# Attention and a low-rank mixer in one kernel: 128-row score operands for heads 0 and 1, two more crossbar transposes, and another order of steps

## The chip, the cores and the metric

The kernel runs on one core of a Trainium2 chip. The metric is the device time of one execution in microseconds, as the median of several runs of the same program. One further execution is recorded by the hardware profiler, and all views of the profile come from that one.

## The reference

The inputs are q, k, v with 8 batches, 8 heads, 576 positions and 64 features in fp32, a signal s for each batch, head and position, and four matrices: U (576x32), V (32x576), w_ch1 (512x2048) and w_ch2 (2048x512). The output is fp32, 8x576x512.

```
scores = q @ k.T / 8                          # per batch and head
cum    = cumsum(max(s, 0))
scores = where(causal, -1e9, scores + min(-(cum[i] - cum[j]), 0))
attn   = softmax(scores);   x = attn @ v      # heads side by side: 512 features
h = x.T @ U @ V                               # over positions, rank 32
u = x + h.T
out = u + max(u @ w_ch1, 0) @ w_ch2
```

## The kernel before

All matmuls are bf16. The work is 64 heads in 32 pairs (a pair is two heads, 128 features of x; a batch has four pairs), and nine groups of 512 tokens for the last two products. The order of all steps is written out by hand: a string `SEQ` of tokens for the first two batches (heads 0 to 15, pairs 0 to 7), whose part ahead of the bar also has warm-up matmuls, and a string `PAIR` that is played once for each pair from 8 on. Each engine executes its own instructions in the order in which the tokens issue them. The loads of the first two batches and the weights go through GpSimd in the order of `LOADS`.

What the tokens stand for, with the lines of the profile:

- `T`, `t` (heads 0 to 15): six TensorE transposes of a head's q and k into PSUM (L219), and two copies of it into the head's operand slot, by ScalarE (`tA`) or VectorE (`tV`) (L231). `G` (four parts for each group of four heads from head 16): VectorE transposes q or k (L245), and after every second part SP issues four copies, one per head, into the slot (L251). A slot holds four heads with 128 rows each: 64 features, four rows for the decays (copied by `R`, L169, or in the opening), and zeros. There are three slots.
- `D`, `E`: the score matmuls of a head on and below the diagonal (L261). For heads 0 and 1 they take 64 rows, and each is followed by a second matmul that adds the decays from another operand (L270). In the first batch a matmul with a triangle of large negative numbers masks the diagonal (L281). `d`, `f`, `m`, `l`: exponentials on ScalarE (L326). `k`, `K`: masks on VectorE by a minimum (L329), from head 8.
- `A`, `a`: attention times v, 15 matmuls (L340), and on VectorE the division (L355, L356).
- For a pair n: `U` multiplies x by U (L370), `u` copies that (L381), `Y` multiplies by V (L423), and `y` writes the piece u = x + h, transposed, into `uT`. x itself must be turned for that. Batches 0 and 1 turn x by matmuls with the identity into the same PSUM tile (`X`, L388, and L409 in `Y`), and `y` is a copy on either engine (L441). From batch 2, `x` turns it by a crossbar transpose that SP issues (L398), and `y` is a VectorE addition (L439).
- `F` feeds one unit of the last two products: `widen(g)` (16 units, each four 512-column matmuls with a tile of w_ch1, L459, and a ReLU by ScalarE, L466) and `narrow(g)` (16 units of four matmuls with w_ch2, L476; after four units one output tile is complete). `Q` puts these units into a queue. `r` does the next due copy: a ReLU, or the final step of an output tile. That final step adds u in token order. For group 0, four matmuls with the identity add it in PSUM (L488) and VectorE copies the tile (L500). For later groups `turn_u` has turned `uT` by a crossbar transpose from SP at the group's first unit (L444), and VectorE adds it (L502). SP then stores the tile (L508).
- `L` is one step of the decays of batches 4 to 7, `Z` clears buffers, `p` issues warm-up matmuls (L547), `e` is a feed that is played from pair 16 on.

In `PAIR` the numbers are relative to the pair: `D0` is the first head of this pair, `A-2` and `A-1` are the heads of the pair before, `U-2` and `Y-2` belong to two pairs before. `G1` works on the group that is used about two pairs later. When the last `y` of a batch is done, the units of that batch's group go into the queue.

PSUM has four buffers for scores and four for all else. Each load of GpSimd and each DMA of SP uses one of eight completion semaphores in turn.

Of the kernel before, what the change touches and what calls it, by code (L numbers as in the profile page):

```python
# [20 lines left out]
def kernel(  # L21
# [236 lines left out]
    def product(h, dst, j, lo, hi, start, stop):  # L258
        bias = bias_0 if h < 2 else None
        rows = D if bias else 128  # L260
        nc.tensor.matmul(  # L261
            dst,
            lhsT=head_of(h)[0:rows, ds(S + j * 128, 128)],
            rhs=head_of(h)[0:rows, lo:hi],
            start=start,
            stop=stop and not bias,
            skip_group_check=True,
        )
        if bias:
            nc.tensor.matmul(  # L270
                dst,
                lhsT=bias[0][:, ds(j * 128, 128)],
                rhs=bias[1 + h][:, lo:hi],
                start=False,
                stop=stop,
                skip_group_check=True,
            )
# [124 lines left out]
    def mix_out(n):  # L402
        mixed = n >= 2 * PB
        cut = 512 - 64 * (n // PB)
# [23 lines left out]
    def mix_done(copy, n):  # L428
        b, hp = divmod(n, PB)
        cut = 512 - 64 * b  # L430
        for got, lo, hi in mix_of.pop(n):
            for p, e in ((lo, min(hi, cut)), (max(lo, cut), hi)):
# [3 lines left out]
                dst = uT[:, at // 512 % 4, hp, ds(at % 512, e - p)]  # L436
                if b >= 2:
                    turned = xT[n % 3].rearrange("p t c -> p (t c)")
# [10 lines left out]
    hidden = {}  # L449
    UB = 1  # L450

    def widen(g):
        if g >= UB:
            turn_u(g)
# [15 lines left out]
    def narrow(g):  # L470
        hT = hidden.pop(g)
        for i in range(4):
            f2 = pwork()
            tok = g * 512 + i * 128
            for nf in range(NF):
# [4 lines left out]
                    start=(nf == 0),  # L480
                    stop=g >= UB and nf == NF - 1,
                    skip_group_check=True,
                )
                if nf % 4 == 3 and nf < NF - 1:
                    pending.append(None)
                    yield
            for dt in range(4 if g < UB else 0):
                nc.tensor.matmul(  # L488
                    f2[:, ds(dt * 128, 128)],
                    lhsT=uT[:, g % 4, dt, ts(i, 128)],  # L490
                    rhs=identity,
                    start=False,
                    stop=(dt == 3),
                    skip_group_check=True,
                )

            def finish(f2=f2, tok=tok, i=i):
                o_sb = work.tile([128, DM], FP32, tag="o_sb", name="o_sb", bufs=3)
                if g < UB:
                    nc.vector.tensor_copy(o_sb, f2)  # L500
                else:
                    nc.vector.tensor_tensor(  # L502
                        o_sb.rearrange("p (d c) -> p d c", d=4),
                        f2.rearrange("p (d c) -> p d c", d=4),
                        u_sb[g % 2][:, :, i, :],
                        op=ALU.add,
                    )
                nc.sync.dma_start(out=out_flat[ds(tok, 128), :], in_=o_sb)  # L508
# [45 lines left out]
    def prepare(i):  # L554
        if i == 0:
            for pT in pTs:
                nc.vector.memset(pT[:, :, 1600:], 1.0)
        elif i == 1:
            nc.vector.memset(slots[2][:D, :, 2 * S :], 0.0)
            nc.vector.memset(slots[2][D:, :, :], 0.0)  # L560
        else:
            nc.vector.memset(slots[0][D:, 0:2, :], 0.0)

    def queue(n):
# [20 lines left out]
        "X": mix_x,  # L585
        "x": turn_x,
        "Y": mix_out,
        "t": take,
# [40 lines left out]
    def opening():  # L629
# [28 lines left out]
        for slot in slots[:2]:  # L658
            nc.vector.memset(slot[:D, :, 2 * S :], 0.0)
        nc.vector.memset(slots[0][D:, 0:2, 2 * S :], 0.0)  # L660
        nc.vector.memset(v_slots[0][:, :, :, D : D + 1], 1.0)
# [49 lines left out]
    def begin_v(i):  # L711
# [14 lines left out]
    LOADS = (  # L726
        "u1 v0 u0 k0 w0 s0 w3 w2 w1 s1 x2 v1 x0 x1 x3 q4 v2 q5 "
    )

    SEQ = (  # L730
        "p7 p5 Z0 T0 tA0 tA0 p8 T3 T1 tA1 T2 tV3 D0 d0 tV3 tV2 tA1 p3 E0 D1 p2 d1 T5 f0 E1 tV2 "
        "m0 T6 f1 D2 T4 | m1 l0 tV5 E2 D3 tV6 d2 E3 f2 tV4 m2 tV4 l1 D4 A1 f3 tV5 A0 d3 E4 d4 "
        "T7 D5 m3 tA6 a1 d5 E5 f4 a0 m4 A2 U0 Z1 f5 m5 A3 D6 R2 uA0 tA7 a2 a3 X0 Y0 l2 tV7 A5 "
        "U1 A4 uV1 yA0 d6 D7 l3 X1 E6 Y1 d7 f6 m6 a4 a5 yV1 E7 U2 f7 A6 uV2 X2 a6 Y2 m7 yA2 A7 "
        "T8 T9 tA8 a7 U3 tV8 uA3 X3 Y3 yV3 D8 Q0 tV9 E8 F tA9 Z2 F d8 r R3 F r F r r T11 F F f8 "
        "r tA11 T10 F Q100 D9 r tV11 tV10 F r T13 k8 E9 T12 m8 F r L tA10 tV12 d9 r l4 k9 tV13 "
        "F K4 tV12 r f9 D10 d10 F F D11 m9 r r E10 f10 m10 l5 F F k10 r tV13 D12 T14 F r E11 "
        "d12 tV14 T15 r tA15 A9 A8 d11 F tV14 f11 k12 tA15 D13 m11 a9 a8 U4 k11 l6 r K5 F uV4 "
        "E12 X4 Y4 A11 f12 m12 E13 r F a11 f13 m13 D14 A10 a10 r D15 F d14 yV4 d13 R4 E14 d15 "
        "U5 F K6 uA5 l7 r X5 E15 k14 f14 F A12 r G4 Y5 k15 F r F k13 A13 f15 m15 a12 r F yA5 K7 "  # L740
        "m14 a13 A15 r U6 r uA6 a15 A14 G4 F r G4 F r F F a14 G4 r U7 F X6 r R5 Y6 L r L yA6 "
        "uA7 L F L F X7 Y7 L r r yA7 Q1 F F Q101 r r F r G5 L G5 L F L r "
    )
    PAIR = (
        "D0 E0 r d0 A-2 U-2 G1 r e k0 F a-2 G1 D1 r A-1 f0 uA-2 e r l0 d1 F m0 a-1 x-1 r F r E1 "
        "f1 k1 Y-2 r e K0 r yA-2 m1 F F "
    )
# [51 lines left out]
```

## Time and profile before

| | us |
|---|---|
| median of 5 runs (373.23 to 376.15) | 375.61 |
| the profiled execution | 376.15 |
| its span | 374.4 |
| TensorE busy | 365.1 |
| ScalarE busy | 210.7 |
| VectorE busy | 193.2 |
| GpSimd busy | 108.5 |

The span runs from the program's first instruction to its last, as the profiler sees it; the execution's own time holds a little more. The chain of work that ended last lies on TensorE for 73% of the span and on DMAs for 17%. A line of the profile names the engine, the line of the kernel, the operation, the tile that is written and the tiles that are read, the shape and the number of such instructions. PE is TensorE, DVE VectorE, ACT ScalarE, POOL GpSimd, SP SyncE.

### The profile page before, as it was taken

What the parts mean: (1) busy time and instruction counts of PE and PEld (TensorE: products, weight loads), DVE (VectorE), ACT (ScalarE), POOL (GpSimd) and SP (SyncE); (2) the same over time, 40 slices, a digit from 0 to 9 for tenths busy, and PEclk for the clock granted to TensorE, in tenths of its full rate; (3) what the DMA queues carried; (4) which work ended last, traced back from release to release, by engine and by line L of the source; (5) the groups of instructions that cost most, each with busy time, mean ns of one, the idle gap of its engine ahead of it and who ended that gap; (6) DMA issues with size and microseconds to landing.
All of it is one profiled execution on the core that took longest, in us unless ns stands there. A gap on an engine that the chain in (4) does not pass through costs nothing.

```text
span 374.4 us, 7894 instructions
## 1 busy us (share of the span) xinstructions
PE 365.1 (98%) x3119; PEld 206.0 (55%) x3119; DVE 193.2 (52%) x406; ACT 210.7 (56%) x429; POOL 108.5 (29%) x175
## 2 busy tenths in 40 slices
PE   8989999998899999999999999999999999999995
PEld 3566566654566565555555555555555544444442
DVE  8487566886478675665476546665343322011011
ACT  7596997178555686347733774377436711611710
POOL 8973338674454274063404400000000000000000
PEclk9999999999899999999999999999999999999999
DMA  7999999999999999869995994363224015005002
GB/s 89 153 196 207 162 164 128 159 182 201 154 140 191 197 149 148 124 125 141 139 149 106 172 115 80 95 161 47 56 76 102 19 46 140 2 28 140 2 28 84
DMA packets 108924, 44.89 MB, mean 120 GB/s; under 512 B 93440, under 2 KB 100640, under 8 KB 108888
## 3 DMA queue, kind: packets, MB, share of 16 engines
q0 software_dynamic: 65616, 18.43, 62.8%
q1 hardware_dynamic: 43272, 25.96, 35.3%
q8 instruction: 24, 0.39, 0.4%
q14 instruction: 12, 0.10, 0.1%
HBM read 37.51 MB, written 10.03 MB: 127 GB/s over the span
## 4 chain that ended last, share of the span: by engine, by line
PE 73%; DMA 17%; POOL 6%; DVE 3%; issue 1%; SPq 0%; DVEq 0%; POOLq 0%
PE pwork L476 29%; PE pwork L459 27%; DMA w_sb<-in_moe_w_ch_dram 10%; PE pscore L261 8%; PE pwork L340 6%; DMA slot<-turned 4%; PE pwork L370 2%; DVE turned L245 2%; POOL v_slot L142 2%; DMA v_slot<-in_v_dram 2%; PE pwork L423 2%; DMA qk_sd<-in_q_dram 1%; POOL hT L116 1%; POOL qk_sd L134 1%; POOL U_sb L691 0%
## 5 line engine op out<-in xcount | busy, mean ns | idle before, releaser
L326 ACT ACTIVATE pT<-pscore 128x512 bf16<-128x512 f32 (+1 forms) x224 | 113.3, 564 | 71.3 <-PE pscore L261 65.8
L459 PE MATMUL pwork<-uT,w_sb 128*128 128x512 bf16 x576 | 133.7, 380 | 0.0
L476 PE MATMUL pwork<-w_sb,hT 128*128 128x512 bf16 x576 | 132.5, 379 | 0.0
L466 ACT ACTIVATE hT<-pwork 128x512 bf16<-128x512 f32 x144 | 85.9, 612 | 55.9 <-PE pwork L459 55.4
L476 PEld LDWEIGHTS <-hT 128*128 128x128 bf16 x576 | 54.5, 98 | 58.1
L459 PEld LDWEIGHTS <-w_sb 128*128 128x128 bf16 x576 | 54.5, 98 | 57.5 <-issue 0.6
L261 PE MATMUL pscore<-slot 128*128 128x128 bf16 (+5 forms) x576 | 64.8, 241 | 3.1 <-DMA slot<-turned 2.3
L502 DVE TENSOR_TENSOR o_sb<-pwork,stage 128x512 f32<-128x512 f32 x32 | 21.9, 686 | 73.8 <-PE pwork L476 70.8
L261 PEld LDWEIGHTS <-slot 128*128 128x128 bf16 (+1 forms) x576 | 40.8, 98 | 32.0 <-DMA slot<-turned 3.1
L245 DVE STREAM_TRANSPOSE turned<-qk_sd 128x576 bf16<-128x576 bf16 x48 | 54.3, 1134 | 0.1
L134 POOL DMA_DIRECT2D qk_sd<-in_q_dram x48 | 27.1, 574 | 77.6 <-DVE turned L245 63.0
L329 DVE TENSOR_TENSOR pT<-pT,keep 128x512 bf16<-128x512 bf16 (+1 forms) x84 | 28.0, 352 | 37.4 <-ACT pT L326 36.1
L340 PE MATMUL pwork<-v_slot,pT 128*128 128x65 bf16 x960 | 40.0, 194 | 0.1
L340 PEld LDWEIGHTS <-pT 128*128 128x128 bf16 x960 | 35.5, 98 | 2.8 <-DVE x_sb L356 0.3
L356 DVE TENSOR_TENSOR x_sb<-pwork,rec 128x320 bf16<-128x320 f32 x64 | 31.5, 492 | 2.2
L439 DVE TENSOR_TENSOR uT<-pwork,stage 128x384 bf16<-128x384 f32 (+7 forms) x48 | 19.8, 452 | 22.1 <-PE pwork L423 14.3
L134 POOL DMA_DIRECT2D qk_sd<-in_k_dram x48 | 27.1, 571 | 11.6 <-DMA v_slot<-in_v_dram 6.1
L142 POOL DMA_DIRECT2D v_slot<-in_v_dram x32 | 28.2, 894 | 3.8 <-DMA w_sb<-in_moe_w_ch_dram 3.4
L355 DVE RECIPROCAL rec<-pwork 128x5 f32<-128x5 f32 x64 | 12.1, 189 | 24.2 <-PE pwork L340 24.0
L231 DVE COPY slot<-pwork 64x576 bf16<-64x576 bf16 x20 | 15.8, 799 | 11.9 <-PE pwork L219 7.3
L370 PE MATMUL pwork<-x_sb,U_sb 128*128 128x128 bf16 x160 | 14.5, 222 | 0.3 <-DVE x_sb L356 0.2
L423 PE MATMUL pwork<-V_sb,ux 128*128 128x512 bf16 (+6 forms) x64 | 13.1, 286 | 0.0
(80 smaller groups left out, 136.9 us busy)
## 6 DMA issues: line engine op xcount, KB each, us to landing
out_dram<-o_sb SPq DMA_DIRECT2D x36, 256.0 KB
slot<-turned SPq DMA_DIRECT2D x96, 72.0 KB
v_slot<-in_v_dram POOLq DMA_DIRECT2D x32, 128.0 KB, 8.8
w_sb<-in_moe_w_ch_dram POOLq DMA_DIRECT2D x8, 512.0 KB, 12.7
qk_sd<-in_q_dram POOLq DMA_DIRECT2D x48, 72.0 KB, 4.0
qk_sd<-in_k_dram POOLq DMA_DIRECT2D x48, 72.0 KB, 5.4
stage<-in_q_dram POOLq DMA_DIRECT2D x2, 288.0 KB, 10.6
stage<-in_k_dram POOLq DMA_DIRECT2D x2, 288.0 KB, 11.4
```

What stands on the lines that cost most here:

```text
L134: nc.gpsimd.dma_start(out=qk_t[g][ds(32 * a, 32), c, :].rearrange("p (n f) -> p n f", n=6), in_=src[g // 2, 4 * (g % 2) + a].rearrange("(n ...
L142: nc.gpsimd.dma_start(out=vt[:, t, :, 0:D], in_=v[b, :, ds(t * 128, 128), :].rearrange("h p d -> p h d"),)
L245: nc.vector.transpose(turned[:, e, c].rearrange("p (n m t) -> p n t m", n=6, t=3), src[:, c].rearrange("p (n t e d) -> p e n t d", n=6, t= ...
L261: nc.tensor.matmul(dst, lhsT=head_of(h)[0:rows, ds(S + j * 128, 128)], rhs=head_of(h)[0:rows, lo:hi], start=start, stop=stop and not bias, ...
L326: nc.scalar.activation(dst, src, EXP, scale=scale)
L329: nc.vector.tensor_tensor(p, p, m, op=ALU.min)
L340: nc.tensor.matmul(po[:, i, :], lhsT=p_of(h)[:, ds(spot(j, i), 128)], rhs=v_slots[h // H % 3][:, j, h % H, :], start=(j == 0), stop=(j == ...
L356: nc.vector.tensor_tensor(x_of[b][:, h % H // 2, :, ts(h % 2, D)], po[:, :, 0:D], rec.to_broadcast([128, 5, D]), op=ALU.mult,)
L370: nc.tensor.matmul(up[:, 0:128], lhsT=U_sb[:, t, :], rhs=x_part(n, t), start=(t == 0), stop=(t == 4), skip_group_check=True,)
L459: nc.tensor.matmul(f1, lhsT=w1_sb[nf // 4][:, kt, ds(nf % 4 * 128, 128)], rhs=uT[:, g % 4, kt, :], start=(kt == 0), stop=(kt == 3),)
L466: pending.append(lambda nf=nf, f1=f1: nc.scalar.activation(hT[:, nf, :], f1, RELU))
L476: nc.tensor.matmul(f2, lhsT=hT[:, nf, ds(i * 128, 128)], rhs=w2_sb[nf // 4][:, nf % 4, :], start=(nf == 0), stop=g >= UB and nf == NF - 1, ...
```

## The change

Four things change together.

Heads 0 and 1 take all 128 rows of their slot for the scores, like the other heads. Their decay rows and the rest are zero, cleared by one larger memset at the start instead of a small one there and a later one (`Z2`). The second matmul with the decays stays.

x of batch 1 is turned by the crossbar (`x4` to `x7`) and added by VectorE; `X4` to `X7` and their part of `Y` go. The pieces of `y` are then 448 and 128 columns wide.

u of group 0 is turned by the crossbar too, with a token of its own, `W0`, and added by VectorE in the final step of the output tile; the matmuls of L488 and the copies of L500 go.

The loads, the steps of the first two batches and those of a pair stand in another order. The front has 22 warm-up matmuls instead of 25 and 37 feeds instead of 35.

```diff
     def product(h, dst, j, lo, hi, start, stop):
         bias = bias_0 if h < 2 else None
-        rows = D if bias else 128
         nc.tensor.matmul(
             dst,
-            lhsT=head_of(h)[0:rows, ds(S + j * 128, 128)],
-            rhs=head_of(h)[0:rows, lo:hi],
+            lhsT=head_of(h)[:, ds(S + j * 128, 128)],
+            rhs=head_of(h)[:, lo:hi],
...
     def mix_out(n):
-        mixed = n >= 2 * PB
+        mixed = n >= PB
...
-                if b >= 2:
+                if b >= 1:
                     turned = xT[n % 3].rearrange("p t c -> p (t c)")
                     nc.vector.tensor_add(dst, got[:, p - lo : e - lo], turned[:, p:e])
...
     def widen(g):
-        if g >= UB:
+        if g > 0:
             turn_u(g)
...
-            for dt in range(4 if g < UB else 0):
-                nc.tensor.matmul(
-                    f2[:, ds(dt * 128, 128)],
-                    lhsT=uT[:, g % 4, dt, ts(i, 128)],
-                    rhs=identity,
...
-                if g < UB:
-                    nc.vector.tensor_copy(o_sb, f2)
-                else:
-                    nc.vector.tensor_tensor(
+                nc.vector.tensor_tensor(
...
-        else:
-            nc.vector.memset(slots[0][D:, 0:2, :], 0.0)
...
+        "W": turn_u,
...
-        nc.vector.memset(slots[0][D:, 0:2, 2 * S :], 0.0)
+        nc.vector.memset(slots[0][D:, 0:2, :], 0.0)
...
-        "u1 v0 u0 k0 w0 s0 w3 w2 w1 s1 x2 v1 x0 x1 x3 q4 v2 q5 "
+        "u0 v0 s0 u1 w2 x2 w0 w1 x0 s1 w3 x3 k0 v1 x1 q5 q4 v2 "
```

In `LOADS`, `v` is v of a batch, `w` and `x` are quarters of w_ch1 and w_ch2, `s` is half of q and k of batch 1, `q` is q and k of a group of four heads, `u0` and `u1` are U and V, `k0` makes the mask.

The front, before and after (the part that the prediction speaks of):

```diff
-"p7 p5 Z0 T0 tA0 tA0 p8 T3 T1 tA1 T2 tV3 D0 d0 tV3 tV2 tA1 p3 E0 D1 p2 d1 T5 f0 E1 tV2 "
-"m0 T6 f1 D2 T4 | m1 l0 tV5 E2 D3 tV6 d2 E3 f2 tV4 m2 tV4 l1 D4 A1 f3 tV5 A0 d3 E4 d4 "
...
-"T8 T9 tA8 a7 U3 tV8 uA3 X3 Y3 yV3 D8 Q0 tV9 E8 F tA9 Z2 F d8 r R3 F r F r r T11 F F f8 "
...
-"d12 tV14 T15 r tA15 A9 A8 d11 F tV14 f11 k12 tA15 D13 m11 a9 a8 U4 k11 l6 r K5 F uV4 "
...
-"uA7 L F L F X7 Y7 L r r yA7 Q1 F F Q101 r r F r G5 L G5 L F L r "
+"p10 T0 p4 Z0 tA0 T1 p5 tA0 T2 T3 tA1 D0 p2 tV2 tA1 E0 d0 D1 f0 tA2 d1 tV3 m0 tV3 p1 E1 "
+"f1 T4 m1 T6 T5 tA6 l0 D2 | E2 D3 A0 tV4 tV5 d2 A1 tV4 tV5 d3 E3 D4 T7 E4 f2 tV6 a0 m2 "
+"f3 m3 l1 D5 d4 A2 f4 E5 m4 d5 f5 A3 a1 Z1 tV7 m5 U0 tV7 uA0 D6 R2 a2 l2 X0 a3 Y0 A4 "
+"yA0 D7 d6 U1 uA1 A5 X1 l3 d7 a4 E6 E7 Y1 a5 yV1 f6 m6 f7 U2 A6 uA2 m7 X2 a6 Y2 A7 a7 "
+"yA2 T8 tA8 U3 uA3 X3 T9 tV8 Y3 D8 yA3 Q0 E8 tA9 T11 F F T10 R3 r F tA9 f8 tV11 r F D9 "
...
+"r d10 r D11 T14 E10 l5 f10 F r tV12 tV13 F d11 tV13 D12 T15 K4 E11 m10 k9 A9 k10 A8 "
+"d12 r D13 tA15 F tV14 r tV14 l6 f11 m11 tA15 a9 k12 a8 U4 K5 F W0 E12 uA4 F k11 r A11 "
...
+"m14 r yV5 x6 G4 r F A15 uA6 G4 R5 F r F A14 r r F Y6 a14 r a15 F x7 L r F G4 r L F F "
+"U7 r r uA7 Y7 F yA6 L yV7 Q1 F L L L r Q101 F r L r F L r F G5 F G5 r "
```

The order of a pair:

```diff
-"D0 E0 r d0 A-2 U-2 G1 r e k0 F a-2 G1 D1 r A-1 f0 uA-2 e r l0 d1 F m0 a-1 x-1 r F r E1 "
-"f1 k1 Y-2 r e K0 r yA-2 m1 F F "
+"G1 A-2 r D0 F r U-2 d0 a-2 k0 r A-1 E0 f0 e D1 l0 r a-1 e x-1 r F E1 e G1 uA-2 Y-2 K0 "
+"r r F yA-2 m0 d1 k1 r f1 F m1 F "
```

## The prediction

> **What bounds the kernel now.** I read the page first, then the chain of waits in order of time, then timelines of TensorE and GpSimd for the places that the chain named.
>
> ```profile
> span 374.4 us, 7894 instructions
> PE 365.1 (98%) x3119; PEld 206.0 (55%) x3119; DVE 193.2 (52%) x406; ACT 210.7 (56%) x429; POOL 108.5 (29%) x175
> PEclk9999999999899999999999999999999999999999
> ```
>
> TensorE is the bound: busy 98%, no other engine over 56%. Busy is not peak, so I count starts. From one start to the next the trace has 0.216 us for 512 columns (the chain: 64 matmuls of L459 in 13.81), 0.190 for 448, 0.137 for 320, 0.082 for 192, 0.056 for 128, 0.028 for 64 or 65, 0.042 for the 96-column transposes. Over all 3119 that is 353.6 us. The span is 374.4: 1.3 before the first matmul, 3.9 after the last start, and 15.6 lost, namely 3.3 before 10 us (cold warm-up matmuls), 3.5 from 10 to 20, 3.5 from 20 to 40, 4.1 from 90 to 100, 1.2 elsewhere. An edit pays if it removes matmuls or some of those 15.6 us.
>
> The loss from 10 to 20, TensorE's timeline:
>
> ```profile
> 9.63 0.23 PE L261 MATMUL pscore<-slot 64*128 64x128 bf16 x1
> 9.79 0.23 PE L270 MATMUL pscore<-hT 128*128 128x128 bf16 x1
> 9.95 0.23 PE L261 MATMUL pscore<-slot 64*128 64x128 bf16 x1
> ```
>
> 64-row products alternate with 128-row bias matmuls, and starts lie 0.16 apart, not 0.056. The loss at 92, and the loads (GpSimd's timeline; a wait there ends when the load issued eight before has landed):
>
> ```profile
> 94.78 1.33 PE L261 MATMUL pscore<-slot 128*128 128x128 bf16 x9 [2.29 <-DMA slot<-turned]
> ...
> 97.26 1.60 PE L459 MATMUL pwork<-uT,w_sb 128*128 128x512 bf16 x4
> ```
> ```profile
> 31.83 0.88 POOL L142 DMA_DIRECT2D v_slot<-in_v_dram  x1 [1.73 <-DMA w_sb<-in_moe_w_ch_dram]
> 34.35 0.69 POOL L146 DMA_DIRECT2D v_slot<-in_v_dram  x1 [1.65 <-DMA w_sb<-in_moe_w_ch_dram]
> ...
> 39.94 0.74 POOL L157 DMA_DIRECT2D w_sb<-in_moe_w_ch_dram  x1 [1.93 <-DMA w_sb<-in_moe_w_ch_dram]
> ...
> 47.42 0.57 POOL L134 DMA_DIRECT2D qk_sd<-in_k_dram  x1 [0.66 <-DMA v_slot<-in_v_dram]
> ```
>
> Head 20's scores wait 2.3 us for their operands, and the next four 512-column matmuls start 0.43 apart: half clock for 3.4 us, 1.7 more. Loads land one after another, a 1 MB weight tile each 2.5 to 2.6 us, and v of batch 1 is complete at 47.14. A9, its first reader, ran at 52.55: 5.4 us of slack.
>
> **Removed matmuls.** x of batch 1 by crossbar: 16 of L388 at 0.056 and 4 of L409 at 0.028, 1.0 us. u of group 0: 16 of L488, 0.9. Warm-up: 22 instead of 25, 0.65. Together **-2.55 us**, all on the bounding engine.
>
> **128 rows for heads 0 and 1.** 18 product and bias pairs lose their 0.1 us steps, up to 3.5 us. The larger memset (64x1216, 1.07 us by the row of L562, instead of 0.11) stands on VectorE ahead of the decays, so the first bias operand comes at 9.4 instead of 8.45; D0 started at 9.63, so scores still begin at about 9.5. But the order then puts A0 ahead of E3 and D4. From D0 to A0 there are 6.1 us of matmuls; ScalarE's copies and exponentials stretch this to about 17.4. A0 needs v of batch 0, which landed at 20.3 and is issued 1.0 us later (U's memset and loads instead of V's): 20.8. The time gained becomes a wait of 3 us on that load. After it come 12.0 us of TensorE steps to the first feed, about 2 more for ScalarE (9.2 us of work up to m7) and the 2.1 us memset Z1 ahead of two copies: first feed at 35.0, before 35.69.
>
> **Load order.** Before v of batch 1 now stand two more weight tiles: 47.14 + 5.15 less what the front differs gives 51.7 (51 to 52.5). A9 stands 14.0 us of matmuls after the first feed (16.9 before), so it is reached at 49.0: a **new wait of 2.3 us** (0 to 3.5). This load then sets the front: through A9 it loses 12.4 us (51.7 - 1.3 - 38.0 of matmuls) where it lost 10.4: **+2.0**. The second tile of w2 lands at about 54, its reader stands at 59: nothing; without that cover each us late costs one.
>
> By the row above, a 2.3 us gap halved the clock; the shorter gaps (up to 0.77) did not. So the wait at A9 may cost 1.7 more; with other new gaps shorter, I put **+0.4**. The Trainium skill, "TensorE: Matmul & The Clock Gate", section "HAM oscillation", gives gaps over about 3.4 us as what throttles; by that the gap at 92 should not have, and A9 would cost no clock, 0.4 less than my sum, but A0's 3 us come near it: a rule that speaks against an order that makes the array wait for loads. The trace's 2.3 decides.
>
> **Sums on VectorE.** Batch 1's y become adds: 4 pairs of 0.615 and 0.287; ScalarE loses three copies. VectorE is busy 29 of 44 us from 35.7 to 80, so the total fits, but not the order: ahead of y7 stand a15, s's scaling 0.56, an output sum 0.69, a transpose 1.13, the scan 1.35 and y6. Group 1's first feed needs y7's first piece in its fourth matmul: **+0.8** (0 to 2.4), where ScalarE's copy came in time. Output sums cost 0.69 as the copies did: nothing.
>
> **New transposes on SP.** W0 can go once T15 has read the stage, near 50, and is read at 62; the row of L444 lands 4.3 to 6.9 after issue. x4 to x7 take 2 to 6 by L398's rows and stand ahead of G4's and G5's copies, with 5 us or more before y4 to y6 need them; y7's has the least, 4. Hidden; uncovered, up to 3 each.
>
> **Head 20's wait.** Group 5's copies stood behind L444, for which SP's queue waited 4.9 us, and L444 landed only at 88.9. Now the second G1 comes after E1, so the last transpose ends near 85.8 while head 20 is due at about 95 (12.7 of matmuls after D16). The measured delay from that transpose to landing, 10.2 (84.45 to 94.64), would leave 0.5 of wait; the shortest row, 1.4 after issue, none. I take 0.3: **-3.8** (-4.1 to 0).
>
> **Feeds.** The front holds 37 feeds, not 35. At pair 13 the queue of 64 units is then empty one feed early, and group 2's first unit follows Y11 with nothing between: **+0.6** (0 to 1.7: Y11 to its first sum by L439's 0.55 with an output sum of 0.69 ahead, less three matmuls). In the other pairs, A-1 needs m1 2 us before its turn and G1's copies have 10.3 us instead of 11.0; the rows from 98 to 147 land 1.5 to 8.7 after issue: nothing.
>
> Sum: -2.55 + 2.0 + 0.4 + 0.8 - 3.8 + 0.6 = **-2.5 us**. The profiled execution took 376.15 (span 374.4, 1.7 around it), so 373.6; the median, 375.61, lies 0.5 lower: **373.1**.
>
> **Rivals.** (1) v of batch 1 lands in time or the front is slower anyway, so A9 doesn't wait: 2.3 less, 370.8. For: 49.0 and 51.7 each carry an error of over 1 us. (2) Head 20 waits as before: 3.8 more, 376.9. For: its lead grows by only 2 us. Against: turn_u no longer waits behind ScalarE. (3) Slower: VectorE becomes the limit where feeds need its sums, at group 1's and group 2's first units. If it runs 1.5 us later than reckoned there, each gap passes 2.3 and brings the half clock: 2 x (1.5 + 1.7) = 6.4, 379.5. For: it takes on 2.6 us of adds in order. Against: 15 us idle in that stretch. (4) 128 rows don't remove the steps: about 2.5 us more before A0, which would still be reached at 19.9, ahead of v's 20.8: 373.1 to 373.4, hardly visible.
>
> **How the numbers follow.** About 0.5% (1.9 us) is what a measurement of this kernel tells from no change; faster means under 373.7. Forecast 0.50, its own range 371 to 375.5: faster 0.29, same 0.20, slower 0.01. Rival 1, 0.17: faster. Rival 2, 0.13: same 0.08, slower 0.05. Rival 3, 0.12: slower. Rival 4, 0.08: faster 0.04, same 0.04. Together faster 0.50, same 0.32, slower 0.18. The range goes down to rival 1 without the 0.8 and 0.6 of the late sums, 369.3, and up to rival 2 with part of the half clock at A9 (0.6 of its 1.7), 377.5.
>
> **What would show it.** L388 at 16, no L488-type identity matmuls, 22 warm-up matmuls; D0's starts 0.056 apart. Right: TensorE idle ahead of A0 until about 20.8 and ahead of A9's last matmuls until about 52, both ended by v_slot loads; no wait for slot<-turned near 95 and full clock there. Wrong: A9 without a wait (then the load or the front was misjudged), a wait at head 20, gaps in the pair loop at every second pair, or new half-clock stretches.

## The result, and the profile after

The changed kernel takes 376.71 us (median of 53 executions, 374.67 to 382.08) where the kernel before takes 375.66 (median of 95). The ratio is 1.0041, 95% interval 1.0029 to 1.0052: slower by 0.4%, where 373.1 and a gain of 0.7% were forecast. The ratio leaves out executions that the chip disturbed, which is why it differs a little from the ratio of the medians. The profiled executions don't show this loss: 375.95 after, 376.15 before.

The page of the changed kernel, its first lines and the chain that ended last:

```profile
span 374.2 us, 7798 instructions
PE 358.7 (96%) x3080; PEld 202.7 (54%) x3080; DVE 197.7 (53%) x405; ACT 209.9 (56%) x425; POOL 108.2 (29%) x175
PEclk9999999999999999999999999999999999999999
PE 78%; DMA 14%; POOL 3%; DVE 2%; issue 1%; ACT 1%; DVEq 0%; POOLq 0%
```

TensorE has 39 matmuls less and is busy 6.4 us less, no slice has a lowered clock, and the span is the same. The removed work has become waiting. Counted from start to start as in the prediction, the steps of all matmuls add up to 351.1 us (353.6 before). The lost time, by stretches of the span:

| stretch, us | lost before | lost after |
|---|---|---|
| 0 to 40 | 10.3 | 10.2 |
| 40 to 60 | 0.2 | 1.8 |
| 60 to 90 | 0.1 | 4.8 |
| 90 to 100 | 4.1 | 0.1 |

The parts that went as predicted come first. TensorE's timeline at the first scores (start, duration, engine, line, operation):

```profile
10.22 0.22 PE L260 MATMUL pscore<-slot 128*128 128x128 bf16 x1
10.28 0.22 PE L269 MATMUL pscore<-hT 128*128 128x128 bf16 x1
10.33 0.22 PE L260 MATMUL pscore<-slot 128*128 128x128 bf16 x1
```

The starts lie 0.056 apart, not 0.16. The same view at A0, at A9 and around head 20:

```profile
17.45 0.65 PE L339 MATMUL pwork<-v_slot,pT 128*128 128x65 bf16 x9
19.46 0.31 PE L339 MATMUL pwork<-v_slot,pT 128*128 128x65 bf16 x5 [1.37 <-DMA v_slot<-in_v_dram]
20.34 0.65 PE L339 MATMUL pwork<-v_slot,pT 128*128 128x65 bf16 x16 [0.56 <-DMA v_slot<-in_v_dram]
...
49.45 1.63 PE L339 MATMUL pwork<-v_slot,pT 128*128 128x65 bf16 x30
...
94.77 0.60 PE L260 MATMUL pscore<-slot 128*128 128x448 bf16 x4
95.21 2.75 PE L457 MATMUL pwork<-uT,w_sb 128*128 128x512 bf16 x12
```

A0 waits for v of batch 0 until 20.3. Head 20's scores at 94.8 have no wait ahead of them, and the matmuls behind them run at full clock. A9 starts at 49.45. Its 30 matmuls take 1.63 us where they took 1.09 before, a wait of only 0.55 us, as v of batch 1 had landed by 50.4.

The part that did not: SP's queue (a line is a DMA issue; the duration is SP's own time for it), VectorE, and TensorE behind them.

```profile
44.46 6.70 SPq L443 DMA_TRANSPOSE stage<-uT  x1
52.41 6.34 SPq L397 DMA_TRANSPOSE stage<-x_sb  x2
```
```profile
62.94 0.82 DVE L438 TENSOR_TENSOR uT<-pwork,stage 128x448 bf16<-128x448 f32 x2 [2.26 <-DMA stage<-x_sb]
...
80.25 0.82 DVE L438 TENSOR_TENSOR uT<-pwork,stage 128x448 bf16<-128x448 f32 x2 [2.69 <-DMA stage<-x_sb]
```
```profile
63.61 0.61 PE L339 MATMUL pwork<-v_slot,pT 128*128 128x65 bf16 x15 [0.91 <-DVE uT L438]
...
80.92 2.32 PE L457 MATMUL pwork<-uT,w_sb 128*128 128x512 bf16 x10 [1.60 <-DVE uT L438]
```

Read from the bottom: group 1's first feed waits 1.6 us for a VectorE addition. VectorE had been idle for 2.69 us, waiting for a transposed x, that is x7. VectorE has no lack of time: it waits for the DMA. x7 was issued by 74.40 and landed at 80.15. The pair of lines at 63 tells the same of x4, which was issued by 53.89 and landed at 62.84, 8.95 us later. W0 stood ahead of it; it occupied SP for 6.7 us and landed at 60.51. By starts, the two waits cost 1.1 and 1.8. The rest of the 4.8 is 0.8 at 77.4, where `Y7` waits for y6 and y6 for its turn on VectorE (x6 had landed at 75.06), 0.9 at 86.1, where scores wait for an exponential, and 0.2 at 72.2.

### The profile page after: what moved, and what is told of

It is laid out like the page before. It is cut to its first block, busy times and chain, and to the rows that moved or that the text cites. A ratio compares the mean times of both kernels' runs of the same rounds, so it can differ in the third digit from the quotient of the medians.

```text
span 374.2 us, 7798 instructions
## 1 busy us (share of the span) xinstructions
PE 358.7 (96%) x3080; PEld 202.7 (54%) x3080; DVE 197.7 (53%) x405; ACT 209.9 (56%) x425; POOL 108.2 (29%) x175
## 4 chain that ended last, share of the span: by engine, by line
PE 78%; DMA 14%; POOL 3%; DVE 2%; issue 1%; ACT 1%; DVEq 0%; POOLq 0%
PE pwork L474 31%; PE pwork L457 29%; PE pscore L260 9%; PE pwork L339 6%; DMA v_slot<-in_v_dram 5%; DMA stage<-x_sb 5%; DMA w_sb<-in_moe_w_ch_dram 4%; PE pwork L369 2%; PE pwork L422 2%; POOL hT L116 1%; POOL v_slot L142 1%; DVE x_sb L355 1%; DVE uT L438 0%; ACT pT L325 0%; DVE o_sb L488 0%
## 5 line engine op out<-in xcount | busy, mean ns | idle before, releaser
L325 ACT ACTIVATE pT<-pscore 128x512 bf16<-128x512 f32 (+1 forms) x224 | 114.9, 566 | 69.3 <-PE pscore L260 68.4
L457 PE MATMUL pwork<-uT,w_sb 128*128 128x512 bf16 x576 | 136.1, 379 | 1.7 <-DVE uT L438 1.6
L474 PE MATMUL pwork<-w_sb,hT 128*128 128x512 bf16 x576 | 135.3, 379 | 0.0
L260 PE MATMUL pscore<-slot 128*128 128x128 bf16 (+4 forms) x576 | 65.8, 240 | 1.6 <-ACT pT L325 1.3
L488 DVE TENSOR_TENSOR o_sb<-pwork,stage 128x512 f32<-128x512 f32 x36 | 24.8, 689 | 75.8 <-PE pwork L474 72.2
L260 PEld LDWEIGHTS <-slot 128*128 128x128 bf16 x576 | 40.4, 98 | 20.6 <-issue 1.8
L134 POOL DMA_DIRECT2D qk_sd<-in_q_dram x48 | 27.1, 574 | 77.4 <-DVE turned L245 34.9
L339 PEld LDWEIGHTS <-pT 128*128 128x128 bf16 x960 | 36.7, 98 | 11.5 <-issue 3.8
L438 DVE TENSOR_TENSOR uT<-pwork,stage 128x448 bf16<-128x448 f32 (+7 forms) x56 | 23.1, 452 | 36.5 <-PE pwork L422 31.5
L380 ACT CAST ux<-pwork 128x128 bf16<-128x128 f32 x32 | 8.5, 264 | 14.4 <-PE pwork L369 14.4
L369 PEld LDWEIGHTS <-U_sb 128*128 128x128 bf16 x160 | 11.3, 98 | 7.9 <-DVE x_sb L355 1.7
```

The costliest lines, as they stand in the source:

```text
L134: nc.gpsimd.dma_start(out=qk_t[g][ds(32 * a, 32), c, :].rearrange("p (n f) -> p n f", n=6), in_=src[g // 2, 4 * (g % 2) + a].rearrange("(n ...
L260: nc.tensor.matmul(dst, lhsT=head_of(h)[:, ds(S + j * 128, 128)], rhs=head_of(h)[:, lo:hi], start=start, stop=stop and not bias, skip_grou ...
L325: nc.scalar.activation(dst, src, EXP, scale=scale)
L339: nc.tensor.matmul(po[:, i, :], lhsT=p_of(h)[:, ds(spot(j, i), 128)], rhs=v_slots[h // H % 3][:, j, h % H, :], start=(j == 0), stop=(j == ...
L457: nc.tensor.matmul(f1, lhsT=w1_sb[nf // 4][:, kt, ds(nf % 4 * 128, 128)], rhs=uT[:, g % 4, kt, :], start=(kt == 0), stop=(kt == 3),)
L474: nc.tensor.matmul(f2, lhsT=hT[:, nf, ds(i * 128, 128)], rhs=w2_sb[nf // 4][:, nf % 4, :], start=(nf == 0), stop=nf == NF - 1, skip_group_ ...
```

## The experiments

Eighteen kernels were run. "Base" is the kernel of before with the 128-row operands and the new pair order. The ratios are to the kernel before, run beside each.

| kernel | median, us | ratio [95%] |
|---|---|---|
| changed kernel | 376.71 | 1.0041 [1.0029, 1.0052] |
| k128: before + 128 rows | 373.90 | 0.9951 [0.9931, 0.9971] |
| k_pair: base | 370.74 | 0.9875 [0.9835, 0.9914] |
| a_xmm: changed, x by TensorE | 374.07 | 0.9983 [0.9943, 1.0023] |
| a_umm: changed, u by TensorE | 375.00 | 0.9985 [0.9961, 1.0008] |
| a_xumm: changed, both by TensorE | 377.21 | 1.0055 [1.0027, 1.0082] |
| a_xumm_l: the same, old loads | 373.37 | 0.9957 [0.9942, 0.9972] |
| a_loads: changed, old loads | 376.94 | 1.0044 [1.0015, 1.0073] |
| a_x4first: changed, x4 ahead of W0 | 375.89 | 1.0012 [0.9989, 1.0035] |
| a_x7mm: changed, x7 by TensorE | 375.26 | 0.9990 [0.9962, 1.0018] |
| a_pair: changed, old pair order | 379.30 | 1.0097 [1.0062, 1.0132] |
| k_pair_l: base, new loads | 372.06 | 0.9896 [0.9858, 0.9935] |
| h_front: base, new steps to Q0 | 371.80 | 0.9912 [0.9881, 0.9943] |
| h_back: base, new steps from Q0 | 372.69 | 0.9933 [0.9911, 0.9955] |
| k_pair_x: base, x by crossbar | 374.19 | 0.9969 [0.9940, 0.9997] |
| k_pair_x456: base, x4 to x6 by crossbar | 371.57 | 0.9895 [0.9867, 0.9923] |
| k_pair_w2: base, u by crossbar | 370.63 | 0.9874 [0.9841, 0.9907] |
| k_pair_w: base, u by crossbar, issued twice | 384.76 | 1.0229 [1.0163, 1.0295] |
| k_pair_wx: the same, and x | 386.12 | 1.0298 [1.0223, 1.0373] |

The theory after the two traces was that the crossbar transposes queue on SP and make the y sums late. The rivals were that the new order itself is slower, or that VectorE is.

**k128.** The 128-row operands alone, in the kernel before (with its `Z2` gone and the larger memset):

```diff
-        rows = D if bias else 128
-            lhsT=head_of(h)[0:rows, ds(S + j * 128, 128)],
+            lhsT=head_of(h)[:, ds(S + j * 128, 128)],
```

> The kernel before with the 128-row operands for heads 0 and 1 alone (larger memset at the start, Z2 gone). Theory: the 0.16 us steps shrink to 0.056 and 3 us come free ahead of 16 us, but the first values (A1) then stand before v of batch 0, which lands near 20.3, so only the 0.9 us by which A1 was later than that are won: ratio to before 0.997 to 1.000. Rival (the front is not held by that load): the whole 3.5 us, ratio 0.991.

The gain was 1.8 us, between the two numbers written down, and in its profile the loss from 10 to 20 us goes from 3.5 to 1.3. Head 20 still waits. TensorE's timeline of this kernel:

```profile
91.97 0.85 PE L260 MATMUL pscore<-slot 128*128 128x128 bf16 x9 [1.80 <-DMA slot<-turned]
...
93.39 1.03 PE L458 MATMUL pwork<-uT,w_sb 128*128 128x512 bf16 x4
```

The wait is 1.8 us, and the four 512-column matmuls behind it take 1.03: full clock. In the profile of before it was 2.29, and the same four took 1.60.

**a_xmm, a_umm, a_xumm.** The changed kernel with x of batch 1, u of group 0, or both given back to TensorE:

```diff
-        mixed = n >= PB                 # a_xmm; X4 to X7 return, x4 to x7 go
+        mixed = n >= 2 * PB
-" ... K5 F W0 E12 uA4 ..."             # a_umm; the identity matmuls of u return
+" ... K5 F E12 uA4 ..."
```

> The changed kernel, with x of batch 1 turned by matmuls again (X4 to X7 right ahead of Y4 to Y7, no x4 to x7). Theory: in the changed kernel VectorE stands behind transposes that land 5 to 9 us after their issue, and TensorE waits for its sums (1.1 at 62, 0.8 at 77, 1.8 at 80 us, and small ones); without them 3 to 4 us of waits go and 1.0 us of matmuls comes back: 373.5 to 374.5, 2 to 3 us under the changed kernel, ratio to before 0.992 to 0.998. Rival (the loads of v hold the front, the waits would only move): 1 us slower than the changed kernel, ratio to before 1.006.

> The changed kernel, with u of group 0 added by TensorE again (no W0). Theory: W0 holds SP's queue until 51 us and lands at 60.5, so x4 behind it lands at 62.8; without W0 x4 lands by 58, y4 is in time, the 1.1 us wait at 62 goes and 0.9 us of matmuls comes back: within 0.5 us of the changed kernel, ratio to before 1.002 to 1.006. The waits for x6 and x7 near 77 and 80 stay. Rival (W0 delays all that follows on the queue): they go too, 2 us or more under the changed kernel.

> The changed kernel with both undone: only the 128-row operands and the new order of steps and loads remain. Theory: like the run with x by matmuls, plus 0.9 us of matmuls: 374.5 to 375.5, ratio to before 0.995 to 1.001. Rival (the order itself is worse): 377 or more, ratio over 1.005.

Each alone adds matmuls of 1.0 and 0.9 us and yet is faster than the changed kernel by 0.6%. In a_umm x4 lands 3.6 us after issue instead of 8.95, and VectorE's timeline has no idle time ahead of y4 and 0.24 ahead of y7:

```profile
63.22 0.82 DVE L438 TENSOR_TENSOR uT<-pwork,stage 128x448 bf16<-128x448 f32 x2
...
80.03 0.82 DVE L438 TENSOR_TENSOR uT<-pwork,stage 128x448 bf16<-128x448 f32 x2 [0.24 <-PE pwork L422]
```

The loss between 60 and 90 us goes from 4.8 to 1.9 in a_umm and 2.2 in a_xmm, and stays at 2.2 with both undone. The 2.2 us of a_xmm are inside the 2 to 3 that were written down. So giving back either set alone removes more waiting than it adds work. Giving back the second one too removes no more waits in that stretch; it costs 2.6 to 2.7 us by the ratios, 0.9 to 1.0 of it matmuls, and what the rest is was not settled. a_umm came out against the number written down for it (it was thought that W0 costs nothing), at its rival's. a_xumm shows that the new order, without any new transpose, is itself slower: 1.0055, although its 128 rows and its pair order are worth 1.25% in the base.

**a_x4first, a_x7mm.** The order of two issues on SP's queue, and pair 7 alone:

```diff
-" ... K5 F W0 E12 ... F f13 x4 D14 ..."    # a_x4first
+" ... K5 F E12 ... F f13 x4 W0 D14 ..."
-" ... a15 F x7 L ... uA7 Y7 ..."           # a_x7mm; pair 7 as in batch 0
+" ... a15 F L ... uA7 X7 Y7 ..."
```

> The changed kernel with two steps exchanged on SP's queue: x4 (the transpose of pair 4's x) goes before W0 (the transpose of group 0's u) instead of behind it; nothing else. Theory (the time goes to late y sums because the new crossbar transposes queue behind each other on SP): in the changed kernel's trace x4 landed 8.95 us after its issue, behind W0, and y4's sum, waiting for it, held TensorE 1.08 us at 62.7; without W0 in the kernel x4 landed after 3.63. So x4 lands near 58, the wait at 62.7 goes, and the kernel comes out 1 us under the changed kernel, 375.7, ratio to before about 1.001 (0.999 to 1.003). Rival (the late y sums are only a symptom of a front that runs late, or of the order of steps on VectorE, and not of SP's queue): the wait moves to W0's reader or to y5, and the time stays within 0.3 us of the changed kernel, ratio 1.004.

> The changed kernel with pair 7's x alone transposed by TensorE as before (4 matmuls more of 0.056 and 1 of 0.028, 0.25 us; y7 copied by ScalarE again). Theory: the wait of 1.76 us at 80.9, where the first feed of group 1 waits for y7's sum, which waits for x7's landing at 80.15, goes, and part of it comes back as matmul time: 1.2 to 1.5 us under the changed kernel, ratio 1.000 to 1.001. Rival (VectorE or the order is what makes y7 late): a wait of over 1 us stays there, ratio 1.003 to 1.005.

Both did what the theory said: 0.3% and 0.5% under the changed kernel. The intervals of a_x4first and the changed kernel still overlap a little; those of a_x7mm and the changed kernel do not. x4 landed 3.9 us after its issue, and the wait at 62 is gone from a_x4first's trace. The profile of a_x4first also shows what else the new front risks. TensorE's timeline around A9, with four 512-column matmuls ahead of it and four behind:

```profile
46.73 1.03 PE L457 MATMUL pwork<-uT,w_sb 128*128 128x512 bf16 x4
...
49.48 0.25 PE L339 MATMUL pwork<-v_slot,pT 128*128 128x65 bf16 x3 [0.48 <-DMA v_slot<-in_v_dram]
50.37 0.28 PE L339 MATMUL pwork<-v_slot,pT 128*128 128x65 bf16 x4 [0.65 <-DMA v_slot<-in_v_dram]
51.83 0.99 PE L339 MATMUL pwork<-v_slot,pT 128*128 128x65 bf16 x21 [1.17 <-DMA v_slot<-in_v_dram]
...
52.94 1.90 PE L457 MATMUL pwork<-uT,w_sb 128*128 128x512 bf16 x4
```

Here the last of v of batch 1 landed at 52.1, 1.7 us later than in the profile of the changed kernel, A9 idled 2.3 us in three pieces (3.0 by starts), and the matmuls behind it ran at half clock (1.90 instead of 1.03).

**a_loads, a_xumm_l, k_pair_l.** One edit, `LOADS` exchanged, in three kernels: in the changed kernel, in a_xumm (both with the old loads), and in the base (with the new ones).

```diff
-        "u0 v0 s0 u1 w2 x2 w0 w1 x0 s1 w3 x3 k0 v1 x1 q5 q4 v2 "
+        "u1 v0 u0 k0 w0 s0 w3 w2 w1 s1 x2 v1 x0 x1 x3 q4 v2 q5 "
```

> The changed kernel with the load order of before (u1 v0 u0 k0 w0 s0 w3 w2 w1 s1 x2 v1 ...). Theory (the front of the changed kernel ends with the load of v of batch 1, which stands behind two more weight tiles; where that load is slow, A9 waits longer): v of batch 1 lands 3 to 5 us earlier, A9 doesn't wait (0.55 us in the changed kernel's profile, 0.8 to 1.2 in the profiles of two variants), half-clock stretches become rarer, and the time is 1 to 2 us under the changed kernel: ratio 0.999 to 1.002. Rival (the front is set by the new order of steps, whatever the loads): the wait at A9 goes but ScalarE's or VectorE's steps behind it set the same time: ratio 1.003 to 1.005. A second rival: the second w2 tile or the first widening tile now comes late for its reader, and the feeds wait: over 1.006.

> The same base with the changed kernel's load order; steps and transposes stay. The base reaches A9 near 50. Theory A (the load order costs: v of batch 1 behind two more weight tiles): v lands at 50 to 53, A9 waits 0 to 2.5 us, the first matmuls of the feeds aren't hit: ratio 0.990 to 0.995. Theory B (the cost of the changed kernel's front lies in its order of steps, since the changed kernel with the loads of before ran at the same 1.004): ratio 0.986 to 0.990.

> The changed kernel with x of batch 1 and u of group 0 on TensorE (377.2 when run) and, besides, the loads of before. Relative to the 128-row kernel with the new pair order (ratio 0.9875), the new steps up to Q0 cost 0.37% alone, the new steps from Q0 on 0.58%, the new loads 0.21%; all three together 1.80%, 0.64% (2.4 us) more than the sum. Theory A (the surplus is new loads against new steps: A9 is reached near 47.5 by the new steps, and the new loads bring v of batch 1 at 50 to 53, where the old loads have it in time): the surplus goes, ratio 0.995 to 0.999. Theory B (the surplus is between the two parts of the new steps, whatever the loads; the changed kernel itself ran at 1.0044 with the loads of before, no better than with its own): ratio 1.002 to 1.006.

The old steps reach A9 at 50.4 and lose 0.2% by the new loads, which is inside the two intervals; the new steps without new transposes lose 1.0% by them (1.0055 against 0.9957). In a_xumm_l's profile TensorE's timeline shows A9's 30 matmuls without a gap:

```profile
48.21 1.09 PE L339 MATMUL pwork<-v_slot,pT 128*128 128x65 bf16 x30
```

But a_loads, with the new transposes, gains nothing; it came out at its rival's number. Its trace shows why: W0 stands at the same place in SP's queue (43.90 to 51.15) and x4 lands at 61.56, so TensorE, early now, waits there and at group 1's first feed as before (0.7 and 1.7 us). The late load and the late transposes limit the same stretch; taking away one leaves the other. With the old loads the price of the transposes shows bare: from a_xumm_l to a_loads they take 1.9 us of matmuls away and the kernel loses 0.87%, 3.3 us.

**k_pair, a_pair.** The new pair order put into the 128-row kernel, and taken out of the changed one:

```diff
-        "D0 E0 r d0 A-2 U-2 G1 r e k0 F a-2 G1 D1 r A-1 f0 uA-2 e r l0 d1 F m0 a-1 x-1 r F r E1 "
-        "f1 k1 Y-2 r e K0 r yA-2 m1 F F "
+        "G1 A-2 r D0 F r U-2 d0 a-2 k0 r A-1 E0 f0 e D1 l0 r a-1 e x-1 r F E1 e G1 uA-2 Y-2 K0 "
+        "r r F yA-2 m0 d1 k1 r f1 F m1 F "
```

> The kernel of before with the 128-row operands (373.9 when run alone) and, besides, the changed kernel's order of the pair loop; front, loads and transposes stay as before. If the new pair order does what the prediction gave it (head 20's wait goes, nothing else in the loop gets worse): the wait of 1.96 us at 89.8 of the 128-row kernel goes, no half-clock stretch follows there, 371.7, ratio about 0.989 (0.987 to 0.991). Rival (the new pair order costs elsewhere in the loop what it gains, or the wait moves to the next loader of group 5): ratio 0.994 to 0.997.

> The changed kernel with the pair order of before. It sizes the one term of the prediction that the two profiles bore out (3.8 us for the end of head 20's wait), now against many executions. In the 128-row kernel the new pair order gained 0.76%, 2.9 us. If it gains as much here: ratio 1.010 to 1.014. If head 20's wait only shows in the profiled execution of before: ratio 1.004 to 1.007.

The order is worth 0.76% (2.9 us) in one and 0.56% (2.1 us) in the other, there between the two numbers written down and nearer the first. Not all of it is head 20. In a_pair's trace TensorE waits at two places where the changed kernel's has almost nothing, ahead of head 20's scores and at group 2's first feed:

```profile
99.40 0.85 PE L260 MATMUL pscore<-slot 128*128 128x128 bf16 x9 [1.34 <-issue]
...
128.92 1.24 PE L457 MATMUL pwork<-uT,w_sb 128*128 128x512 bf16 x5 [2.19 <-DVE uT L438]
```

The second is the wait that the prediction feared under "Feeds"; k128 has one of 1.0 us there. What ended the first the profile does not tell. In the base, TensorE's timeline has almost nothing left of head 20's wait:

```profile
92.01 0.41 PE L260 MATMUL pscore<-slot 128*128 128x128 bf16 x5 [0.29 <-DMA slot<-turned]
```

It is not gone for good: in k_pair_l, which has the new pair order too, this wait was 1.7 us.

**h_front, h_back.** Both orders have done the same steps when they reach Q0, so the halves can be exchanged in the base:

```diff
-SEQ = old order up to Q0 + old order from Q0
+SEQ = new order up to Q0 + old order from Q0     # h_front
+SEQ = old order up to Q0 + new order from Q0     # h_back
```

> The kernel of before with 128-row operands, the new pair order and the loads of before (370.74 when run; x of batch 1 and u of group 0 stay with TensorE), and the changed kernel's order of steps up to Q0 (batch 0: both orders hold the same steps up to there; 22 warm-up matmuls instead of 25); the steps from Q0 on as before. Together with its mirror image it splits the cost of the new order, which stands at some 5 us (all of the new order but the transposes: 377.2; of it the load order 1.3). Theory A (the new order of batch 0 asks for v of batch 0 at A0, waits for it and loses the clock behind it): 1.5 to 3 us over the base, ratio 0.991 to 0.996. Theory B (batch 0's order is as good, and the cost stands behind Q0): within 0.7 us of the base, ratio 0.986 to 0.990.

> The mirror image: the order of before up to Q0, the changed kernel's order of steps from Q0 to the pair loop (x of batch 1 and u of group 0 with TensorE), loads of before. Theory A (A0 and its clock are most of the cost): 1 to 2 us over the base, ratio 0.990 to 0.993. Theory B (the cost stands behind Q0: the waits of 0.4 to 1.1 at 52, 55, 79 and 87 in the profiles with the new order): 2.5 to 5 us over the base, ratio 0.994 to 1.001.

They cost 0.37% and 0.58%; both theories had put most of it in one half, and by these numbers it is in both. The intervals of h_front and the base overlap, so the first is not clear of nothing. With the new loads' 0.21% that makes 1.16%, and all three together cost 1.80%. The base's own 0.4% stands in each of these numbers, so the difference, 2.4 us, is rough. Its place is firmer: a_xumm_l has the same steps as a_xumm and the old loads, and costs 0.82%, so it is loads against steps.

The largest wait that the new steps from Q0 bring in h_back's trace, 1.1 us by starts, comes from the order of two steps on ScalarE. TensorE and ScalarE:

```profile
75.25 0.38 PE L387 MATMUL pwork<-identity,x_sb 128*128 128x128 bf16 x4 [0.96 <-ACT uT L440]
```
```profile
74.38 0.27 ACT L380 CAST ux<-pwork 128x128 bf16<-128x128 f32 x1 [8.92 <-PE pwork L369]
74.54 0.77 ACT L440 CAST uT<-pwork 128x448 bf16<-128x448 f32 x3
```

The new order issues `uA7` ahead of `yA6`. ScalarE was idle for 8.9 us until u7 could run, with y6 behind it, though `Y6` had run near 70; and X7 waited for y6.

**k_pair_x, k_pair_x456, k_pair_w2.** The transposes alone, in the base, where no other part of the change is near them:

```diff
-        mixed = n >= 2 * PB                # k_pair_x; x4 to x7 behind the last divide of each pair
+        mixed = n >= PB                    # k_pair_x456: and n != 7
-        if g >= UB:                        # k_pair_w2, with UB = 0 and W0 behind K5 F
+        if g > 0:
             turn_u(g)
```

> The same base, and x of batch 1 by crossbar DMA without W0; x4 to x7 are issued right behind the last divide of their pair. Theory: 16 matmuls of 0.056 and 4 of 0.028 go, 1.0 us; each x lands 3 to 6 us after issue, which leaves y4 to y6 in time, and y7 the least: a wait of 0 to 1.8 at group 1's first feed: 369.7 to 371.5, ratio 0.985 to 0.989. Rival (the queue of SP is full with scores' operands there, whatever W0 does): waits of over 2 us in sum at y4 to y7: ratio 0.991 or more.

> The base with x of pairs 4, 5 and 6 by crossbar DMA, and pair 7's by TensorE. With all four the base went from 370.74 to 374.19: TensorE waited 2.4 us at 75.4 for y7's sum and lost the clock behind it, and 1.0 at 65. Theory (pair 7's transpose is the one with no slack): 0.75 us of matmuls go, the wait at 75.4 and the half clock go, the 1.0 at 65 stays: 370.5 to 371.5, ratio 0.986 to 0.989. Rival (each of the four costs, as the transposes are slower than the order allows for anyway): 372 or more, ratio 0.990 or more.

> The base with u of group 0 by crossbar DMA (W0 at the place in the order that the changed kernel gives it), x of batch 1 with TensorE. In the earlier kernel for this question turn_u(0) ran twice, once already at the first widening, and the first of the two took the stage buffer that TensorE's transposes waited for, 11.0 us; here it runs once. Theory (a transpose costs only what queues behind it): 16 matmuls of 0.056 go, no wait comes: 369.9, ratio 0.985 (0.982 to 0.988). Rival (W0 holds SP's queue for the operands of scores, or holds the stage for K and Q of batch 2): 371.5 or more, ratio 0.989 or more.

All four x lose 0.94% (3.4 us) where they take 1.0 us of matmuls away, the rival's number. Three of them still lose 0.8 us by the medians, inside the two intervals, and u loses nothing and gains nothing, though its 0.9 us of matmuls are gone. In k_pair_x, VectorE and TensorE at group 1's first feed:

```profile
77.44 0.82 DVE L438 TENSOR_TENSOR uT<-pwork,stage 128x448 bf16<-128x448 f32 x2 [2.80 <-DMA stage<-x_sb]
```
```profile
78.11 3.73 PE L458 MATMUL pwork<-uT,w_sb 128*128 128x512 bf16 x9 [2.36 <-DVE uT L438]
```

x7 landed 4.7 us after its issue; TensorE waited 2.4 and then took 3.73 for nine matmuls, which is half clock. In k_pair_x456 the remaining wait is at y5 (1.6 us; x5 landed 7.0 after issue). In k_pair_w2 W0 stood on SP for 7.7 us and landed 9.0 later, and nothing waited for it. But VectorE waited for x of pair 8, which landed 7.7 us after its issue, and TensorE for the sum, where the base has no wait:

```profile
98.34 0.82 DVE L438 TENSOR_TENSOR uT<-pwork,stage 128x384 bf16<-128x384 f32 x2 [3.57 <-DMA stage<-x_sb]
```
```profile
98.95 0.61 PE L339 MATMUL pwork<-v_slot,pT 128*128 128x65 bf16 x15 [0.61 <-DVE uT L438]
```

With 0.3 us more at head 20 this is as much as u's matmuls took. That W0 is the reason was not shown.

**k_pair_w, k_pair_wx.** The first try at u in the base had only `UB = 0` and the token W0. The first `widen` then called `turn_u(0)` as well, and W0 called it again.

> The kernel of before with 128-row operands and the new pair order (370.74 when run), and u of group 0 by crossbar DMA (W0 at the place in the order that the changed kernel gives it); x of batch 1 stays with TensorE, so no small transpose stands behind W0 on SP. Theory (the crossbar transposes cost only through what queues behind them): 16 matmuls of 0.056 go, 0.9 us, and no wait comes: 369.9, ratio 0.985 (0.982 to 0.988). Rival (W0 also delays the operands of scores that share SP's queue, or its own reader waits): ratio 0.988 to 0.993.

> The same base with both, x4 ahead of W0 and x5 behind it: all the matmuls that the change removes but the warm-up ones are gone (1.9 us). If the transposes' cost is only their queue: y4's wait is gone, y5's is 0 to 0.5, y7's 0 to 1.8: 368.9 to 371, ratio 0.982 to 0.988. Rival: the waits come back as in the changed kernel (4 us and more in sum from 60 to 90): ratio 0.992 or more.

The first of the two transposes took the stage buffer ahead of batch 1's q and k. The waits of TensorE in k_pair_w (us in total, times, longest):

```profile
PE pwork L219 <- DMA stage<-uT: 11.0, 1, 11.0
```

These two say nothing on the theory, but price a transpose that takes a buffer at a time when TensorE needs it.

**The version that beats both** is the base, k_pair: 370.74 us, 1.25% under the kernel before and 1.6% under the changed one. It keeps the first of the four parts of the change and, of the fourth, the order of a pair. k_pair_w2, at 370.63, is the same within its interval.

## Why the prediction was wrong

**Removed matmuls, -2.55: right as a sum of steps** (353.6 to 351.1), and worth much less as time. Of the 1.9 us of transposes among them, 0.5 arrives in the changed kernel (a_xumm to the changed kernel, 0.14%), none or less in the base.

**New transposes, "Hidden": the first step that failed.** The prediction let x4 to x7 take 2 to 6 us by L398's rows. x4 took 8.95, x5 5.15, x6 6.17, x7 5.75. Two readings were wrong. The rows themselves spread wider: in the trace of before L398's land 1.2 to 8.3 us after issue, and the first seven of L444 2.3 to 10.2; 2 to 6 and 4.3 to 6.9 are the first few of each. And the times were not added: the prediction knew that W0 goes ahead of x4 in one queue, yet didn't add W0's time to x4's. W0 itself took 9.4. a_x4first shows this second part alone.

**Sums on VectorE, +0.8: mis-sized, and by the wrong cause.** From 60 to 90 us 4.7 more is lost than before, 2.9 of it at y4 and y7. There the limit is the DMA ahead of the sum; VectorE idles 2.3 and 2.7 us. Only the 0.8 at y6 is VectorE's order, as reckoned for y7. The row for y7 gave x7 a slack of 4 us, and the landings of x7 after issue in the changed kernel, a_umm, a_x4first, k_pair_x, a_loads, a_pair and k_pair_wx were 5.8, 3.3, 4.7, 4.7, 5.8, 3.3 and 4.0 us: a slack of 4 is inside their spread. Rival 3 (slower, from VectorE's sums at group 1's and group 2's first units) had the right place and sign for group 1, not the right engine; group 2's unit did not wait.

**Front, +2.0: the second step that failed; about right in the one trace, wrong in split, and too small over many executions.** Through 60 us the trace loses 1.5 more than before. A0's wait of 2.5 was expected (3). At A9 the trace has 0.55 where 2.3 were predicted; the traces of a_xmm, a_x7mm, a_xumm, a_umm, a_x4first and a_pair, with the same loads and the same steps up to there, have 0.5, 1.0, 1.2, 1.3, 3.0 and 4.2. What a landing time does in one execution is a sample; the old order's slack of 5.4 us hid the spread, and the new one passes it on. The cost of new loads with new steps, 1.0% (3.7 us) without the transposes, is more than the whole term.

Which of the two steps weighs more depends on which is taken away first. Without the new transposes (a_xumm) the terms that are left, -0.65, 2.0, 0.4, -3.8 and 0.6, give -1.45, and 2.1 slower was measured; the transposes then took about 0.5 off, inside the two intervals, where -1.9 and 0.8 make -1.1. So put, the error is in the front and the pair loop. With the old loads the transposes cost 3.3, and so put it is in them. Each hides the other.

**Half clock, +0.4: about right in size, too narrow in place.** The changed kernel's profile has no half-clock stretch behind a gap. But each execution lists its mean granted clock. 17 of 30 executions of before (those in the first comparison) have full clock, 0.998 or more; 16 of 52 of the changed kernel do. The mean is 0.9961 and 0.9948, which makes 0.5 us.

The prediction charged only A9 and called the other new gaps shorter, though its own forecast for A0 was 3 us. Seven traces have the new loads with the new steps, and six of them have a half-clock stretch there: a_xmm and a_x7mm (3.4 us) and a_umm and a_xumm (6.8) at A0, a_x4first and a_pair (3.4) at A9. Only the changed kernel's own has none. The three with the new steps up to Q0 and the old loads (a_loads, a_xumm_l, h_front) have none either, nor have those with the old steps up to Q0 but for k_pair_w and k_pair_wx with their wait of 11 us. So a part of what new loads cost with new steps is clock: the mean of a_xumm is 0.9934 beside 0.9961 for before, that of a_xumm_l 0.9978 beside 0.9978, about 1.0 of the 3.8 us between the two. This is a sum over the listed clocks and not a run of its own.

**Head 20, -3.8: right in the traces (-4.0), too large in the times.** The whole pair order is worth 2.9 and 2.1 us. The profiled execution of before was one with a half-clock stretch, which cost 1.7 us behind the 2.3 us wait; more than half of its executions have none. And the new pair order brings a wait of 0.9 of its own, scores behind an exponential at pair 9 (86.1 here, 79.4 in k_pair), where the prediction had nothing. The full-clock executions have a median of 374.4 before and 375.9 after. So the base of the sum was too high by about the clock's share. That, and that the changed kernel's profiled execution is one at full clock, is why the two profiles look equal while the times differ. In the traces the parts add up: -2.5 for matmuls, 1.5 up to 60 us, 4.7 from 60 to 90 and -4.0 around head 20 make -0.3, and the spans differ by -0.2.

**Feeds, +0.6:** 0.05 in the trace; the new pair order kept the wait away, which came to 2.2 in a_pair without it. **128 rows:** as predicted, the steps go (rival 4 did not come), and alone they give 1.8 us, which the new order's A0 gives up again (from 10 to 20 us k128's trace loses 1.3 and the changed kernel's 3.6). **Not seen at all:** the smaller waits that the new steps bring behind Q0 (0.4 at 51.8 and 0.3 at 55.3, where `U4` and `Y4` or `X4` come too soon for VectorE and ScalarE, and 0.8 to 1.1 near 77, `X7` or `Y7` behind y6), which h_back prices at 2.2 us.

What stays open: what makes a load or a transpose land 1 to 3 us later in one execution than in another, and whether and why the new steps up to Q0 lose 0.4% with the old loads too; h_front's profile is as short as the base's (369.4 against 369.3), so the loss shows only over its six executions.

## What to carry to other kernels

Before moving work from the bounding engine to a DMA, compare the distance of its consumer with the DMA's slowest landing, not with its first few, and add up all that stands ahead of it in the same queue. Here a matmul transpose of 0.25 us was cheaper than one that landed 3 to 9 us after its issue and whose consumer the prediction put 4 to 5 us away. Size a gain from many executions where the profile has a half-clock stretch in it, as one profile is one sample. And when several edits are tied together in one order, try them apart: the 128 rows and the order of a pair were worth 1.25%, and the rest took 1.7% back. The Trainium skill, "VectorE: DVE Perf Modes", section "Rules for kernel authors", says for a 128x128 transpose to use TensorE where PSUM can be the destination and the crossbar otherwise; k_pair_x agrees, with a loss of 0.94% for leaving TensorE; k_pair_w2, where u left it, neither lost nor gained.

## What was not expected of the hardware

A crossbar transpose of 128x640, x of batch 1, landed 1.4 to 9.0 us after SP had issued it, and the larger one of u stood on SP for 1.7 to 7.7 us. The one of x4 took 8.95 behind W0 (changed kernel) and 3.9 ahead of it (a_x4first).

Waits that halve the clock need not be one gap. Single waits of 1.8 (k128) and 1.7 (k_pair_l) at head 20 left it alone, 2.3 (before) and 2.4 (k_pair_x) halved it for 3.4 us, and 2.2 (group 2's first feed in a_pair) left it alone. Several waits with short work between them did so too:

| trace, place | waits, us | half clock, us |
|---|---|---|
| changed kernel, A0 | 1.37, 0.56 | none |
| a_x7mm, A0 | 1.51, 0.39 | 3.4 |
| a_xmm, A0 | 1.24, 0.72 | 3.4 |
| a_umm, A0 | 1.25, 1.90 | 6.8 |
| a_xumm, A0 | 0.31, 1.58, 0.73 | 6.8 |
| a_x4first, A9 | 0.48, 0.65, 1.17 | 3.4 |
| a_pair, A9 | 1.46, 1.85 | 3.4 |

The first three rows have almost the same waits and not the same clock, so the sum of the waits alone does not decide. The Trainium skill, "TensorE: Matmul & The Clock Gate", section "HAM oscillation", names gaps over about 3.4 us; in these traces shorter ones suffice, and the traces decide.
